# Two weight loads of the boot tied to a matmul, and 27 fewer spare instructions ahead of the first turn

## The chip, the cores and the metric

The kernel runs on one core of a Trainium2 chip. The core has a matmul engine (TensorE, PE in the profile, with its weight loads listed apart as PEld), VectorE (DVE), ScalarE (ACT), GpSimd (POOL), and SyncE (SP), which here only issues transfers. Sixteen DMA engines move the data that these engines ask for. The metric is the device time of one execution in microseconds; lower is better.

## The reference

Two blocks follow each other. The first is a linear recurrence over 768 steps for each of 4 x 8 heads of width 48, with a decay w for each channel:

```python
for t in range(S):
    cur = np.einsum('bhd,bhe->bhde', u[None] * kt, vt)
    y[:, :, t] = np.einsum('bhd,bhde->bhe', rt, state + cur)
    state = wt[:, :, :, None] * state + np.einsum('bhd,bhe->bhde', kt, vt)
```

Its output, as 3072 tokens of 384 numbers, goes through a layer of 2048 hidden units, all in float32:

```python
h = x @ w_in
g = h - np.tanh(h)
return g @ w_out
```

## The kernel before

The tokens are cut into eight blocks of 384 (four batches, two halves of the sequence). Within a block the recurrence is worked out by chunks of 64 steps: products of the decays by scans on VectorE (`behind` L387, `before` L376), scores within a chunk (`own`) and their decayed part (`earlier`) as small matmuls at L447, states from one chunk to the next (`update_1` L521 on TensorE, `update_2` L533 and L543 on VectorE), and then the block's result, from the scores (`from_scores`, L603) and from the states (`from_states`, L586). `result_out` (L636) copies the result to three tiles xT and one tile `late`, the fourth part, whose rows are then spread into holes that the three xT tiles have: six small transfers of 24 KB, called fills here (`fill_holes`, L643, `xT<-late`), three on SP's queue and three on GpSimd's for the first block, and all six on SP's for the others.

The second block of the reference then runs over 16 steps f: `hp` (L749, three matmuls of 128x384) makes the hidden values of 128 units, ScalarE copies them to `h` (L752), VectorE squares them (L778) or ScalarE does, two VectorE operations give g (L755, written to `sums` or `g`), and L826 or L864 multiplies with w_out into the accumulators `acc`. In the steps of one block, the recurrence of the next block is prepared, and the weights are converted: in the first block each of 16 pieces of weights arrives as 768 KB of 64-bit numbers (`raw`, L241), ScalarE takes three operations on it (L255) and VectorE one (L259). There are five buffers for `raw`.

Ahead of all this stands the boot (L963 to L1033), which does the recurrence of the first block alone, with nothing of the second block to fill TensorE. Its order on TensorE, ScalarE, VectorE and SP is the order of the code, written out by hand. The steps that matter here:

- SP first issues the loads of w, k and r in two halves, v, and three pieces of weights (L241).
- `turn` (L463 on) takes a number `ahead`: so many spare 16x16 matmuls (`passed`, L277), each two instructions, a weight load and a matmul, stand ahead of its six transposes (L471). The first turn has 97 of them. Nothing reads what they write.
- The fourth and fifth pieces of weights are the two loads of the change. Here the fourth is tied by `begin_behind` to the third of ScalarE's conversions of the first piece (`first_a[2]`, L255): SP's transfer waits for that operation. The fifth has no tie of its own and follows on SP's queue.
- `own`'s scores are masked by VectorE (L454), and `from_scores` for the first pair of heads follows on TensorE (L603, 48 matmul records).
- The first copies to `late` release the fills; `later.load("w")`, the next block's w, is tied to the first copy to xT2 and stands on SP's queue behind the three fills; the sixth piece of weights and the next block's k follow it.
- The fourth piece is converted from the end of the boot on (L255, at 27.63 us in the profile), the fifth in step f = 1 (at 33.30).

In the first steps of the loop, VectorE squares the first h (L778), scans the next block's w (L387), and then does the two operations L755 for the first g.

Of the kernel before, what the change touches and what calls it, by code (L numbers as in the profile page):

```python
# [50 lines left out]
B, H, S, D = 4, 8, 768, 48  # L51
P = 128
L = 64
# [3 lines left out]
NCP = NCH // 2  # L57
# [63 lines left out]
def kernel(  # L121
# [12 lines left out]
    nc = tc.nc  # L134
# [29 lines left out]
    start = const.tile([P, UP * NCH * LP], F32, name="start", tag="start")  # L164
# [32 lines left out]
    A = const.tile([P, 2, NPAIR, NCP, L], F32, name="scores", tag="scores")  # L197
# [41 lines left out]
    def load_weights(f, queue):  # L239
        raw = conv.tile([P, 2 * DM, 2], I32, name="raw", tag="raw")  # L240
        ins = queue.dma_start(out=raw, in_=weights[f].bitcast(I32).rearrange("p (n two) -> p n two", two=2))  # L241
        return f, raw, ins

    def convert(f, raw, _):

        lo, hi = raw[:, :, 0], raw[:, :, 1]
        a = w_sb[:, f, :].bitcast(I32)
        up = conv.tile([P, 2 * DM], I32, name="up", tag="up", bufs=4)  # L250
        low, high = (up.bitcast(t).rearrange("p (n two) -> p n two", two=2)[:, :, i]
                     for i, t in enumerate((U16, F16)))

        def scaled(to, of, scale, bias=0.0):
            return lambda: nc.scalar.activation(out=to, in_=of, func=AF.Copy, scale=scale, bias=bias)  # L255

        return [scaled(a.bitcast(F32), hi.bitcast(F32), HIGH_SCALE), scaled(high, hi.bitcast(F32), SIGN_SCALE),
                scaled(low, lo.bitcast(U32), *LOW)], [
                lambda: nc.vector.scalar_tensor_tensor(out=a, in0=a, scalar=3, in1=up, op0=ALU.logical_shift_left,  # L259
                                                       op1=ALU.bitwise_or)]  # L260

    def scratch(ps):
        return ps.tile([P, 2, BANK], F32, name="att", tag="att")

    def busy(to, n):

        by = ident.bitcast(BF16)
        for _ in range(n):
            nc.tensor.matmul(to, lhsT=by[:, 0:P], rhs=by.unsqueeze(1).to_broadcast([P, 2, 2 * P]), start=True,
                             stop=True, skip_group_check=True)  # L270
# [10 lines left out]
    class Block:  # L281
# [177 lines left out]
        def own(self, ps, p0):  # L459
            return self.masked(ps, "k", "r", masks["diagonal"], p0)  # L460

        def earlier(self, ps, p0):
            return self.masked(ps, "post", "pre", masks["above"], p0)  # L463
# [129 lines left out]
        def from_scores(self, yp, slots, first, last):  # L593
            for n, slot in slots:
                for p in reversed(slot):
                    for c in range(NCP):
                        for h in range(2):
                            for par in range(2):
                                toks = slice(64 * par, 64 * par + 64)
                                e0 = 64 * (h ^ (p % 2))  # L600
                                f0 = p * D2 + h * D
                                n0 = (n * NCP + c) * L
                                nc.tensor.matmul(yp[p % 2][e0:e0 + D, par, n0:n0 + L],  # L603
                                                 lhsT=self.v[toks, c, f0:f0 + D],
                                                 rhs=A[toks, h, p, c, :],
                                                 start=(first and n == slots[0][0] and c == 0),
                                                 stop=(last and (n, c) == (slots[-1][0], NCP - 1)),
                                                 skip_group_check=True)

        def results(self, ps):  # L610
            self.yp = [scratch(ps) for e in range(2)]
# [2 lines left out]
        def result(self, part, pairs, last=False, more=False, **how):  # L614

            if self.begun and not self.more:
                nc.tensor.wait_ge(fence, len(fences))
            slots = [(p // 2, [x for x in pairs if x // 2 == p // 2]) for p in pairs if p % 2 == 0]  # L620
            getattr(self, part)(self.yp, slots, not self.begun, last, **how)
            self.begun, self.more = True, more
            if not last and not more:
                nc.tensor.drain().then_inc(fence, 1)
                fences.append(None)

        def result_out(self, pairs, copy=None):

            copies = []
            for p in reversed(pairs):  # L630
                n = p // 2
                src = self.yp[p % 2][:, :, n * NCP * L:(n + 1) * NCP * L].rearrange("e a (c t) -> e c a t", t=L)
                dst = self.xT[p] if p < KC else self.late
                dst = dst.rearrange("e (c a t) -> e c a t", a=2, t=L)
                for rows in (slice(0, D), slice(64, 64 + D)) if copy else (slice(0, P),):
                    copies.append((copy or nc.scalar.copy)(out=dst[rows], in_=src[rows]))  # L636
            return copies[0]
# [108 lines left out]
    def first(xT, f, ps):  # L746
        hp = ps.tile([P, NB], F32, name="hp", tag="hp")
        for kc in reversed(range(KC)):
            nc.tensor.matmul(hp, lhsT=w_in_sb[:, f, kc, :], rhs=xT[kc],  # L749
                             start=(kc == KC - 1), stop=(kc == 0))  # L750
        h = dense.tile([P, NB], F32, name="h", tag="h")
        return h, nc.scalar.activation(out=h, in_=hp, func=AF.Copy, scale=1.0 / UPSCALE)  # L752
# [199 lines left out]
    def more_weights(queue):  # L952
        raws.append(load_weights(more_weights.n, queue))
        more_weights.n += 1
        return raws[-1][-1]
# [3 lines left out]
    def begin_behind(ins, dma):  # L959
        tc.add_manual_dep(dma.ins, ins.ins.name, mybir.DependencyInfo(  # L960
            mybir.DependencyClass.Sync, mybir.DependencyReason.DATA))

    def boot(ps, blk, later):  # L963
        h1, h2 = HALVES
        for p0 in HALVES:
            for name in ("w", "k", "r"):
                blk.load(name, p0, UP)
        blk.load_v()
        for _ in range(3):
            more_weights(nc.sync)  # L970

        def run(ops):
            for op in ops:
                op()

        both = (h1, h1 + 1), (h2, h2 + 1)
        blk.behind(h1, UP)
        blk.take_whole(h1, UP)
        blk.before(h1, UP)
        blk.times_behind(h1, UP)  # L980
        blk.times_u(h1, UP)
        blk.turn(ps, h1, ahead=97)
        own = blk.own(ps, h1)
        blk.times_before(h1, UP)
        earlier = blk.earlier(ps, h1)
        blk.bound(h1)
        blk.bound(h2)
        blk.behind(h2, UP)
        blk.take_whole(h2, UP)
        own()  # L990
        blk.times_behind(h2, UP)
        blk.times_u(h2, UP)
        blk.turn(ps, h2)
        own = blk.own(ps, h2)
        earlier()
        blk.before(h2, UP)
        blk.times_before(h2, UP)
        blk.update_1(ps)
        first_a, first_b = convert(*raws.pop(0))
        second_a, second_b = convert(*raws.pop(0))  # L1000
        third_a, third_b = convert(*raws.pop(0))
        run(first_a[:2])
        begin_behind(first_a[2](), more_weights(nc.sync))
        more_weights(nc.sync)
        own()
        blk.results(ps)
        blk.result("from_scores", both[0])
        blk.update_2()
        run(second_a)
        blk.result("from_states", ALL, cs=(0, 1), more=True)  # L1010
        earlier = blk.earlier(ps, h2)
        run(third_a[:2])
        blk.result("from_states", ALL, cs=(2,))
        earlier()
        idle = scratch(ps)[:, 0]
        busy(idle, 2)
        blk.result_out((3,), nc.scalar.copy)
        blk.fill_holes([nc.sync, nc.gpsimd])
        begin_behind(blk.result_out((2,), nc.scalar.copy), later.load("w"))
        more_weights(nc.sync)  # L1020
        run(first_b)
        blk.result("from_scores", both[1], True)
        busy(idle, 5)
        run(third_a[2:])
        blk.result_out((1,), nc.scalar.copy)
        blk.result_out((0,), nc.vector.tensor_copy)
        later.load("k")
        fourth_a, fourth_b = convert(*raws.pop(0))
        run(fourth_a[:1])
        run(second_b)  # L1030
        run(third_b)
        blk.held(0, NPAIR)
        return fourth_a[1:], fourth_b  # L1033
# [24 lines left out]
    for i, blk in enumerate(blocks):  # L1058
# [11 lines left out]
        phases, before, ahead, converted, loads = plan(i)  # L1070
# [3 lines left out]
        for f in range(NF):  # L1074
# [5 lines left out]
            h, made = first(here, f, ps_d)  # L1080
# [161 lines left out]
```

## Time and profile before

| | us |
|---|---|
| runs | 567.37, 567.84, 567.37 (median 567.37) |
| the profiled execution | 567.05 |
| its span, first to last instruction | 565.2 |
| boot: first hp (L749) begins | 27.87 |
| first unbroken stretch of TensorE begins (L826) | 40.72 |
| granted TensorE clock, mean | 0.999 |

The costliest groups of the page, with their line, engine, operation, output and inputs, count, busy us, mean ns of one, and the idle time before them:

```profile
L749 PE MATMUL hp<-xT,w_sb 128*128 128x384 f32 x768 | 270.1, 488 | 2.0 <-ACT h L752 1.4
L864 PE MATMUL acc<-forms,g 128*128 128x128 f32 x810 | 121.0, 277 | 0.5
L796 DVE TENSOR_TENSOR g<-g 128x256 f32<-128x256 f32 x225 | 95.4, 424 | 19.1 <-PE acc L864 0.5
```

TensorE sets the pace of the loop, and idles only a few microseconds of it. The boot is the part in which all engines wait for each other and for transfers. `SPq` in a row is SP's queue: the time that it took to issue a transfer, not the transfer's own. An instruction row with `x6` merges six neighbours, and a matmul of float32 is two records of weight load and two of matmul.

### The profile page before, as it was taken

How to read it: one execution, taken by the hardware profiler on the slowest of the kernel's cores; microseconds unless marked ns; L12 is line 12 of the kernel's file. 1: busy time of each engine (PE TensorE's matmuls, PEld its weight loads, DVE VectorE, ACT ScalarE, POOL GpSimd, SP SyncE). 2: the span in 40 equal slices, each digit the busy share in tenths (PEclk: the TensorE clock that was granted, in tenths of full speed). 3: DMA queues.
4: the chain of work that ended last, by engine and by line, in shares of the span. 5: the costliest groups of instructions: out<-in, count | busy, mean ns of one | idle time of the engine just before them, and what ended most of it. 6: DMA issues, size and time to landing. Idle time of an engine off the chain costs nothing.

```text
span 565.2 us, 13965 instructions
## 1 busy us (share of the span) xinstructions
PE 546.4 (97%) x5664; PEld 398.3 (70%) x5664; DVE 477.3 (84%) x926; ACT 376.8 (67%) x743; POOL 11.8 (2%) x40
## 2 busy tenths in 40 slices
PE   4889999999999999999999999999999999999996
PEld 4646666565665787877777777877877787787863
DVE  8888884799879989989999999989899998758673
ACT  3979893355337886588766886677865886566450
POOL 6100000000000000000000000000000000000000
PEclk9999999999999999999999999999999999999999
DMA  8596553244202532035302531126122320100101
GB/s 305 198 337 210 182 174 119 84 112 106 92 12 97 131 111 67 4 97 143 112 22 76 140 114 60 52 86 156 57 68 81 83 64 1 55 1 1 44 0 45
DMA packets 51268, 55.10 MB, mean 97 GB/s; under 512 B 21376, under 2 KB 49152, under 8 KB 51200
## 3 DMA queue, kind: packets, MB, share of 16 engines
q1 hardware_dynamic: 50960, 54.10, 31.6%
q8 instruction: 45, 0.74, 0.5%
q14 instruction: 23, 0.19, 0.1%
q0 software_dynamic: 96, 0.07, 0.1%
q10 hardware_dynamic: 144, 0.00, 0.0%
HBM read 43.55 MB, written 4.72 MB: 85 GB/s over the span
## 4 chain that ended last, share of the span: by engine, by line
PE 87%; DVE 6%; ACT 3%; DMA 2%; issue 1%; SPq 0%; DVEq 0%
PE hp L749 40%; PE acc L864 20%; PE acc L826 13%; PE att L864 5%; PE att L447 3%; PE att L586 2%; PE att L603 2%; PE att L521 2%; DVE g L796 1%; ACT up L255 1%; DMA r<-in_rT 1%; DMA w<-in_wT 1%; PE att L471 1%; DVE g L755 1%; DVE post L401 1%
## 5 line engine op out<-in xcount | busy, mean ns | idle before, releaser
L749 PE MATMUL hp<-xT,w_sb 128*128 128x384 f32 x768 | 270.1, 488 | 2.0 <-ACT h L752 1.4
L749 PEld LDWEIGHTS hp<-xT,w_sb 128*128 128x128 f32 x768 | 138.4, 190 | 81.8 <-ACT h L752 4.5
L752 ACT ACTIVATE h<-hp 128x384 f32<-128x384 f32 x128 | 62.8, 490 | 116.4 <-PE hp L749 114.7
L864 PE MATMUL acc<-forms,g 128*128 128x128 f32 x810 | 121.0, 277 | 0.5
L864 PEld LDWEIGHTS acc<-forms,g 128*128 128x128 f32 x810 | 109.1, 192 | 16.9 <-issue 1.2
L796 DVE TENSOR_TENSOR g<-g 128x256 f32<-128x256 f32 x225 | 95.4, 424 | 19.1 <-PE acc L864 0.5
L755 DVE SCALAR_TENSOR_TENSOR h<-h,s 128x384 f32<-128x384 f32 x128 | 70.3, 549 | 7.2 <-ACT s L770 6.6
L826 PE MATMUL acc<-w_sb,sums 128*128 128x384 f32 x192 | 68.1, 491 | 1.4 <-DVE sums L755 1.1
L755 DVE SCALAR_TENSOR_TENSOR g<-qa,h 128x384 f32<-128x384 f32 x96 | 53.6, 558 | 16.2 <-PE acc L864 2.7
L771 ACT ACTIVATE qa<-s,shift 128x384 f32<-128x384 f32 x90 | 55.4, 616 | 3.0
L773 ACT ACTIVATE junk<-s,shift 128x384 bf16<-128x384 f32 x90 | 54.0, 599 | 0.0
L826 PEld LDWEIGHTS acc<-w_sb,sums 128*128 128x128 f32 x192 | 35.7, 190 | 25.8 <-DVE sums L755 2.2
L770 ACT ACTIVATE s<-h 128x384 f32<-128x384 f32 x90 | 47.1, 523 | 2.8
L864 PE MATMUL acc<-w_sb,g 128*128 128x128 f32 x270 | 44.9, 275 | 0.0
L864 PEld LDWEIGHTS acc<-w_sb,g 128*128 128x128 f32 x270 | 37.4, 192 | 0.0
L781 ACT ACTIVATE qa<-s,shift 128x384 f32<-128x384 f32 x38 | 23.4, 617 | 19.3 <-DVE top L778 19.3
L255 ACT ACTIVATE up<-raw 128x768 f16<-128x768 f32 (+1 forms) x32 | 32.0, 1070 | 0.0
L755 DVE SCALAR_TENSOR_TENSOR sums<-qa,h 128x384 f32<-128x384 f32 x32 | 17.9, 558 | 15.6 <-ACT qa L781 12.4
L778 DVE CUSTOM_DVE_ANT_0 s<-h 128x384 f32<-128x384 f32 x38 | 21.0, 553 | 11.7 <-ACT h L752 11.7
L864 PE MATMUL att<-w_sb,g 128*128 128x128 f32 x180 | 30.2, 275 | 0.0
L864 PEld LDWEIGHTS att<-w_sb,g 128*128 128x128 f32 x180 | 26.4, 192 | 4.5
L387 DVE TENSOR_TENSOR_SCAN post<-w,seed 128x780 f32<-128x780 f32 x16 | 28.5, 1783 | 0.7 <-DMA w<-in_wT 0.6
(90 smaller groups left out, 549.3 us busy)
## 6 DMA issues: line engine op xcount, KB each, us to landing
raw<-in_weights SPq DMA_DIRECT2D x16, 768.0 KB, 4.4
w<-in_wT SPq DMA_DIRECT2D x7, 780.0 KB, 4.5
k<-in_kT SPq DMA_DIRECT2D x7, 768.0 KB, 4.4
r<-in_rT SPq DMA_DIRECT2D x7, 768.0 KB, 4.4
v_sb<-in_v SPq DMA_DIRECT2D x8, 576.0 KB, 4.3
k<-in_tokens SPq DMA_DIRECT2D x6, 576.0 KB, 3.9
r<-in_tokens SPq DMA_DIRECT2D x6, 576.0 KB, 4.8
out_y<-sums SPq DMA_DIRECT2D x15, 128.0 KB, 1.9
```

The source lines that it names most:

```text
L255: return lambda: nc.scalar.activation(out=to, in_=of, func=AF.Copy, scale=scale, bias=bias)
L387: return nc.vector.tensor_tensor_scan(out=back(t[:, 0:width]), data0=back(self.tile("w")[:, a:a + width]), data1=back(seed[:, 0:width]), i ...
L749: nc.tensor.matmul(hp, lhsT=w_in_sb[:, f, kc, :], rhs=xT[kc], start=(kc == KC - 1), stop=(kc == 0))
L752: return h, nc.scalar.activation(out=h, in_=hp, func=AF.Copy, scale=1.0 / UPSCALE)
L755: return lambda: nc.vector.scalar_tensor_tensor(out=out, in0=in0, scalar=scalar, in1=in1, op0=op0, op1=ALU.mult)
L770: nc.scalar.activation(out=s, in_=h, func=AF.Square)
L771: nc.scalar.activation(out=qa, in_=s, func=AF.Square, bias=shift[:, 4:5])
L773: nc.scalar.activation(out=junk[:, 0:NB], in_=s, func=AF.Relu, bias=shift[:, 5:6], accum_out=excess[:, at:at + 1])
L781: first = [lambda: nc.scalar.activation(out=qa, in_=s, func=AF.Square, bias=shift[:, 4:5])]
L796: return lambda: nc.vector.tensor_tensor(out=G[:, to:to + 2], in0=two(G, g_at(q, a0), g_at(q, a1)), in1=two(G, g_at(q, b0), g_at(q, b1)), ...
L826: nc.tensor.matmul(acc, lhsT=g[:, j * P:(j + 1) * P], rhs=w_out_sb[:, f, :], start=(f == self.first), stop=(f == NF - 1))
L864: nc.tensor.matmul(to, lhsT=G[:, g_at(q, a), :], rhs=rhs, start=start, stop=stop, skip_group_check=True)
```

## The change

The tie of the fourth weight load goes from ScalarE's third conversion to the last matmul of the first `from_scores`; for that, `from_scores` and `result` now return their last matmul. ScalarE's three conversions are the same ones in the same place. The two loads stand at the same place of SP's queue: behind the first three pieces, ahead of the fills. The first turn has 70 spare matmuls in place of 97.

```diff
-                                nc.tensor.matmul(yp[p % 2][e0:e0 + D, par, n0:n0 + L],
...
+                                done = nc.tensor.matmul(
+                                    yp[p % 2][e0:e0 + D, par, n0:n0 + L], lhsT=self.v[toks, c, f0:f0 + D],
...
+            return done
...
-            getattr(self, part)(self.yp, slots, not self.begun, last, **how)
+            done = getattr(self, part)(self.yp, slots, not self.begun, last, **how)
...
+            return done
...
-        blk.turn(ps, h1, ahead=97)
+        blk.turn(ps, h1, ahead=70)
...
-        run(first_a[:2])
-        begin_behind(first_a[2](), more_weights(nc.sync))
-        more_weights(nc.sync)
+        run(first_a)
         own()
         blk.results(ps)
-        blk.result("from_scores", both[0])
+        begin_behind(blk.result("from_scores", both[0]), more_weights(nc.sync))
+        more_weights(nc.sync)
```

In the built program TensorE has 54 instructions fewer, all of them ahead of the first turn, and the other engines have as many as before. On SP the fourth weight load waits for TensorE's counter in place of ScalarE's; the next block's k load, which named TensorE's counter too, no longer does, as the wait further up covers it.

More of the change, by code (lines that the diff above doesn't have):

```diff
@@ L602, in from_scores @@
                                 n0 = (n * NCP + c) * L
[L603 to L608, printed above, removed]
+                                done = nc.tensor.matmul(
+                                    yp[p % 2][e0:e0 + D, par, n0:n0 + L], lhsT=self.v[toks, c, f0:f0 + D],
+                                    rhs=A[toks, h, p, c, :], start=(first and n == slots[0][0] and c == 0),
+                                    stop=(last and (n, c) == (slots[-1][0], NCP - 1)), skip_group_check=True)
+            return done
         def results(self, ps):
```

## The prediction

> **What bounds the kernel now.** I read the page's totals first, then busy time by stage, then the chain of waits through the boot, then the order of time around the change.
>
> ```profile
> PE 546.4 (97%) x5664; PEld 398.3 (70%) x5664; DVE 477.3 (84%) x926; ACT 376.8 (67%) x743; POOL 11.8 (2%) x40
> ...
> q8 instruction: 45, 0.74, 0.5%
> ```
>
> ```profile
> 27.30:31.90 4.60, 3.86 (x13) 2.09 (x13) 2.63 (x7) 3.00 (x5) 0.00 (x0) 1.00 0.78 251
> 31.90:41.00 9.10, 7.85 (x25) 3.95 (x24) 8.36 (x13) 7.70 (x11) 0.00 (x0) 1.00 1.02 379
> 41.00:559.00 518.00, 515.25 (x5048) 376.29 (x5048) 441.52 (x865) 348.27 (x702) 0.80 (x12) 1.00 0.29 83
> ```
>
> From 41 us to the end TensorE is busy 515.25 of 518.00 us (first figure after each length) at a granted clock of 1.00. What happens there costs at most the 2.75 us left; everything else is decided by the moment at which that unbroken stretch starts. That moment is 40.72 us, and it is set by this chain:
>
> ```profile
> 27.29 4.54 DMA w<-in_wT
> ...
> 31.85 1.79 DVE post L387
> ...
> 40.11 0.57 DVE sums L755
> ...
> 40.72 2.20 PE acc L826 x6
> ```
>
> The load of the next block's w leaves SP at 27.29 and lands at 31.83; VectorE scans it (L387), and then works almost without a gap to the `sums` that L826 waits for. So a shift of L387's start is a shift of the end. The rows around the change:
>
> ```profile
> 17.39 1.97 ACT L255 ACTIVATE up<-raw 128x768 f16<-128x768 f32 x2
> 19.64 1.46 PE L603 MATMUL att<-scores,v_sb 64*48 64x64 f32 x48
> 24.57 2.61 SPq L643 DMA_DIRECT2D xT<-late  x3
> 27.29 0.52 SPq L330 DMA_DIRECT2D w<-in_wT  x1
> 27.87 2.17 PE L749 MATMUL hp<-xT,w_sb 128*128 128x384 f32 x6 [0.54 <-DMA xT<-late]
> 30.65 0.56 DVE L778 CUSTOM_DVE_ANT_0 s<-h 128x384 f32<-128x384 f32 x1 [1.30 <-ACT h L752]
> 31.85 1.78 DVE L387 TENSOR_TENSOR_SCAN post<-w,seed 128x780 f32<-128x780 f32 x1 [0.64 <-DMA w<-in_wT]
> ```
>
> L387 has two gates. One is the w load (31.83). The other is L778, ahead of it on VectorE, done at 31.21: it needs the first h, hence the first hp (27.87), hence the six small transfers xT<-late (the fills). The second gate has 0.64 us to spare.
>
> **The spare instructions.** 97 took 2.58 us, 27 ns each, so 27 fewer end 0.7 us sooner, at 3.9 instead of 4.65. TensorE then idles until 9.20, where it waits for VectorE's post (L401): gain 0. Without that idle stretch it would be 0.7. They leave no colder clock: the six turns of L471 take 1.54 us after 4.55 us of idling and 1.54 us again at 14.30 after 0.8.
>
> What they do change is where TensorE's instructions are fetched. The 45 packets of queue q8 are 0.74 MB, 16.4 KB each, and TensorE has 11,328 records: some 252 instructions a packet. Counting the built program's instructions against the packets' times, a packet starts about 1.05 us after TensorE has reached a place some 60 short of a multiple of 256. Each spare pair is two instructions, so every fetch comes 54 instructions later in the program. Fetch 4 was asked for near 22.4 us (L586) and will be near 22.8; fetch 5 moves from 30.8 past 40. [...] Here TensorE indeed never waits for one, but SP does:
>
> ```profile
> L643 SPq DMA_DIRECT2D xT<-late x3: 588/640/1297, 24.6 to 26.6; - x3
> ```
>
> ```profile
> q8 instruction: 1, 0.02, 57.6%
> ```
>
> The second line is from the DMA view of 25.2 to 25.3 us. The packet records give fetch 4 from 25.241 to 26.162; SP's second fill was issued at 25.252 and took 1.297 us where the median of 45 fills is 0.582. The same stretch to about 1.29 us recurs at 94.79 and 486.34, each with an instruction packet, and each ends 0.36 to 0.39 after the packet. So fetch 4 costs SP 0.715 us ahead of the w load.
>
> **The tie.** The fourth weight load was issued at 19.384, as ScalarE's third conversion ended (19.36). It will wait for the last of L603's 48 matmuls, 19.64 + 1.46 = 21.10; add the same 0.03: 21.13, later by 1.75. The fifth follows behind it. Behind both on SP stand the three fills, the w load, the sixth weights and k; SP is free again near 21.95, before the first fill's own release (24.54), so the queue's order costs nothing. The two loads landed at 23.89 and 25.75 and will land near 25.6 and 27.5; they are used at 27.63 and 33.30, so 2 and 5.8 us of cover hold, and 1.75 eats most of the first.
>
> **What they collide with.** DMA was 97% busy from 21.5 to 24.7. Fetch 4 waited 2.85 us from its asking and began 4 ns after its engine had finished its last weight packet. Its engine's fills come behind it: by the trace's landing records their last parts came at 27.44 (first SP fill), 27.26, 27.62 and 27.80 (GpSimd's), 1.1 to 1.6 after the fetch's end, and the first hp began 0.22 after 27.62, level with ScalarE's last xT copy (27.61). With the loads 1.75 later and fetch 4 asked for only 0.4 later, I expect it behind both loads again: start 25.24 + 1.75 = 26.99, end 27.92, fills from that engine near 29.1. No row shows this arrangement, so I bound it. If the engine's loads keep the whole 1.75, the first hp moves by 1.75. If they finish 0.5 earlier (fetch 3, which ran into their first packets at 20.14, moves to about 21.0, ahead of them) and queued fills follow each other in 0.35, it moves by 1.0. I take 1.4, nearer the upper row because that one is this very engine's.
>
> At the same time the second fill loses its 0.715 (the fetch is later), so w may leave at 26.58 and land near 31.1; if the fetch holds w's own issue to 27.92 + 0.37 = 28.29, it lands 4.02 after that (27.81 to 31.83): 32.3.
>
> **The sum.** L778 ends at 31.21 + 1.4 = 32.61, behind w in either case, so L387 starts 32.61 - 31.85 = 0.76 later. VectorE's stretch to `sums` is unchanged, and TensorE's own hps (over at 39.62, 1.10 of slack) are not in the way: +0.76. Against the profiled execution, span 565.2 and 1.85 around it, 567.05 becomes 567.81. The median of the runs is 0.32 above that execution: 567.37 + 0.76 = **568.1**. The bounds 1.0 and 1.75 give +0.36 to +1.10: 567.7 to 568.5.
>
> Later collisions are not charged. Fetches move by 0.4 to 5 us there, some onto other blocks' fills, but the stretch at 94.79 left no gap in TensorE at 98, where those fills are used.
>
> **Rivals.**
> 1. *The fetch slips between the two loads.* Fetch 4, at its engine near 23.85, goes between loads four and five: 24.9 to 25.8. The second fill is held as before (to 26.2) and w leaves near 26.9. That engine's share of load five, 8 packets of 234 ns, then ends near 27.7, its fills near 28.1, and they land 0.35 after that: hp later by about 0.65, L778 ends at 31.86: +0.01, 567.4. For it: fetch 4 did begin at an end of a load. Against it: fetch 5 was asked for near 30.8 and began at 34.67, deep in the k load, after a whole weight load and most of k; some 32 of an engine's packets passed first. [...]
> 2. *Nothing holds the fills (faster).* Fetch 4 is served in its usual 1.05 us, as fetches outside loads are. Then hp stays with ScalarE's copy at 27.61, SP gains its 0.715, and L387 starts at L778's end: -0.62, 566.75. For it: every fetch in a quiet stretch. Against it: fetch 1, with a wait of 3.5 in the first loads.
> 3. *The same, and the unexplained gap before `sums` goes too.* VectorE idles 0.56 at 34.31, and the profile names no wait; fetch 5 begins at 34.67 beside it and moves away. -0.62 - 0.56 = -1.18: 566.2. Only closeness in time speaks for it.
> 4. *The w load is caught instead of the second fill (clearly slower).* If the fetch's packet begins between 26.58 and 27.10, it holds w's issue itself; with the longest packet seen (1.43, at 305.3) behind a load end of 26.99, SP is free at 28.79, w lands at 32.81, and the fills of that engine land near 29.8, hp +2.1, L778 33.31: +1.0 to +1.5, 568.4 to 568.9. It decides once hp is later by more than 1.77. For it: my own start, 26.99, lies in that window. Against: the usual packet takes 1.0.
>
> **How the numbers follow.** Forecast 0.42; rival 1: 0.14; 2: 0.10; 3: 0.08; 4: 0.26. A measurement here can tell 0.2% (1.13 us) from no change: below 566.24 is faster, above 568.50 slower. Faster: rival 3 and 0.04 of rival 2, 0.12. Slower: rival 4, and 0.08 of the forecast for what its bounds leave out above, 0.34. Same: 0.34 + 0.14 + 0.06 = 0.54. For 8 in 10 the range runs from 566.4 (rival 2 in, most of 3 out) to 569.1 (rival 4 in, with 0.2 for its rounding); the forecast's own is 567.7 to 568.5.
>
> **What would show it.** Right: the two weight loads issued near 21.13; a q8 packet starting near 27 rather than 25.24; no second fill of 1.29; the first hp later by 1.0 to 1.75; L387 released by L778, not by w; the L826 gap ending near 41.5; the stretch after it unchanged. A q8 packet at 24.9 is rival 1; one at 23.9 with hp at 27.9, rival 2; that and no gap ahead of the first `sums`, rival 3; L387 waiting for w at 32.8, rival 4. Wrong altogether: an end that moves by another amount than L826's start.

## The result, and the profile after

| | before | after |
|---|---|---|
| runs on the same chip, median of 6 | 567.76 (567.37 to 568.30) | 571.12 (570.93 to 571.65) |
| ratio, 95% interval | | 1.0061 [1.0048, 1.0074] |
| the profiled execution | 567.05 | 571.19 |
| its span | 565.2 | 569.5 |
| first hp (L749) begins | 27.87 | 32.32 |
| first unbroken stretch of TensorE begins (L826) | 40.72 | 44.53 |

The change costs 3.4 us; 568.1 was forecast, and the time lies above the range (566.4 to 569.1). The two profiled executions are 4.14 apart because that of before is 0.7 faster than its median.

The page of the changed kernel, its totals and the fetch queue, which has as many packets as before:

```profile
PE 547.2 (96%) x5637; PEld 397.9 (70%) x5637; DVE 477.5 (84%) x926; ACT 376.9 (66%) x743; POOL 11.3 (2%) x40
...
q8 instruction: 45, 0.74, 0.5%
```

TensorE is busy 0.8 us longer with 27 matmuls fewer: something made it slower. Busy time by stage of the changed kernel (length, then busy us of PE, PEld, DVE, ACT, POOL, the granted clock, the DMA share, GB/s):

```profile
22.00:24.00 2.00, 1.01 (x55) 0.77 (x45) 1.87 (x4) 2.00 (x3) 0.13 (x2) 1.00 0.88 326
24.00:26.00 2.00, 0.00 (x0) 0.00 (x0) 0.96 (x2) 0.03 (x1) 0.00 (x0) 0.69 0.94 377
26.00:28.00 2.00, 1.29 (x25) 0.81 (x24) 0.00 (x0) 0.47 (x1) 0.00 (x0) 0.50 0.15 61
28.00:31.00 3.00, 2.91 (x52) 1.64 (x51) 0.43 (x1) 2.88 (x6) 1.58 (x3) 0.50 0.18 45
31.00:35.00 4.00, 3.81 (x12) 1.50 (x10) 2.60 (x5) 1.90 (x5) 0.00 (x0) 0.93 0.72 215
35.00:45.00 10.00, 9.17 (x28) 4.93 (x29) 9.16 (x17) 9.03 (x14) 0.00 (x0) 1.00 1.00 372
45.00:563.00 518.00, 515.16 (x5048) 376.36 (x5047) 441.43 (x863) 348.31 (x702) 0.79 (x12) 1.00 0.30 83
```

The long stretch at the end is what it was (515.16 of 518 us). New are two stages: from 24 to 26 TensorE does nothing at all, and from then to 31 its granted clock is 0.50. The order of time there:

```profile
20.24 0.54 PE L603 MATMUL att<-scores,v_sb 64*48 64x64 f32 x21 [0.49 <-issue]
20.83 0.80 SPq L241 DMA_DIRECT2D raw<-in_weights  x2
26.58 0.89 PE L586 MATMUL att<-pre,states 48*48 48x64 f32 x23 [3.46 <-issue]
28.52 2.23 SPq L643 DMA_DIRECT2D xT<-late  x3
30.86 0.52 SPq L330 DMA_DIRECT2D w<-in_wT  x1
32.32 2.17 PE L749 MATMUL hp<-xT,w_sb 128*128 128x384 f32 x6
35.10 0.56 DVE L778 CUSTOM_DVE_ANT_0 s<-h 128x384 f32<-128x384 f32 x1 [1.45 <-ACT h L752]
35.65 1.78 DVE L387 TENSOR_TENSOR_SCAN post<-w,seed 128x780 f32<-128x780 f32 x1
44.53 0.91 PE L826 MATMUL acc<-w_sb,sums 128*128 128x384 f32 x2 [0.56 <-DVE sums L755]
```

In the middle of L586, between the 9th and the 10th of its last 32 matmul records, TensorE stands still for 3.46 us. `<-issue` says that no semaphore that the profile shows ended the wait: no engine and no data transfer of the kernel. The chain of waits has the same hole, and behind it the way that the prediction followed:

```profile
23.12 3.46 issue
26.58 0.92 PE att L586 x23
...
30.44 1.77 PE att L269 x5
...
32.32 2.19 PE hp L749 x6
...
35.10 0.56 DVE s L778
...
35.67 1.78 DVE post L387
...
43.92 0.57 DVE sums L755
...
44.53 1.56 PE acc L826 x4
```

The sum of it: L586 ends at 26.58 + 0.89 = 27.47, before at 22.81 + 0.66 = 23.47: 4.00 later. Of this 3.46 are the hole; the rest is that its records took 1.57 in two parts instead of 0.66, less 0.37 by which TensorE was ahead when it began them. Another 0.45 come up to hp, where the five spare matmuls of L269 take 1.84 instead of 1.25 at a granted clock of 0.50: hp +4.45. L778 follows it, +4.45; L387 had 0.64 to spare and slips by 3.80; L826 by 3.81. The last 0.43 of the span's 4.24 come later, in the loop.

### The profile page after: what moved, and what is told of

Its sections match the earlier page's. It is cut to its first block, busy times and chain, and to the rows that moved or that the text cites. A ratio compares the mean times of both kernels' runs of the same rounds, so it can differ in the third digit from the quotient of the medians.

```text
span 569.5 us, 13910 instructions
## 1 busy us (share of the span) xinstructions
PE 547.2 (96%) x5637; PEld 397.9 (70%) x5637; DVE 477.5 (84%) x926; ACT 376.9 (66%) x743; POOL 11.3 (2%) x40
## 4 chain that ended last, share of the span: by engine, by line
PE 86%; DVE 8%; issue 2%; ACT 1%; DMA 1%; SPq 0%; DVEq 0%; ACTq 0%
PE hp L749 40%; PE acc L864 19%; PE acc L826 13%; PE att L864 5%; PE att L447 2%; PE att L586 2%; PE att L603 2%; PE att L521 2%; DVE g L796 1%; DMA r<-in_rT 1%; DVE states L533 1%; DVE states L543 1%; DVE g L755 1%; DVE pre L394 1%; DVE post L401 1%
## 5 line engine op out<-in xcount | busy, mean ns | idle before, releaser
L749 PE MATMUL hp<-xT,w_sb 128*128 128x384 f32 x768 | 270.1, 488 | 1.6 <-ACT h L752 1.4
L749 PEld LDWEIGHTS hp<-xT,w_sb 128*128 128x128 f32 x768 | 138.4, 190 | 81.3 <-ACT h L752 4.5
L796 DVE TENSOR_TENSOR g<-g 128x256 f32<-128x256 f32 x225 | 95.5, 424 | 19.1 <-PE acc L864 0.5
L826 PE MATMUL acc<-w_sb,sums 128*128 128x384 f32 x192 | 68.0, 490 | 0.8 <-DVE sums L755 0.6
L826 PEld LDWEIGHTS acc<-w_sb,sums 128*128 128x128 f32 x192 | 35.7, 190 | 25.1 <-DVE sums L755 1.2
L778 DVE CUSTOM_DVE_ANT_0 s<-h 128x384 f32<-128x384 f32 x38 | 21.0, 553 | 11.8 <-ACT h L752 11.8
L376 DVE TENSOR_TENSOR_SCAN pre<-w,start 128x780 f32<-128x780 f32 x16 | 28.5, 1783 | 0.6
```

Source lines behind the costliest of these rows:

```text
L376: return nc.vector.tensor_tensor_scan(out=self.tile("pre")[:, cols], data0=self.tile("w")[:, cols], data1=start[:, 0:n * NCH * LP], initia ...
L796: return lambda: nc.vector.tensor_tensor(out=G[:, to:to + 2], in0=two(G, g_at(q, a0), g_at(q, a1)), in1=two(G, g_at(q, b0), g_at(q, b1)), ...
L826: nc.tensor.matmul(acc, lhsT=g[:, j * P:(j + 1) * P], rhs=w_out_sb[:, f, :], start=(f == self.first), stop=(f == NF - 1))
```

## What the packets of instructions show

The instruction packets (queue q8) carry 16.4 KB each. In the changed kernel 256 records of TensorE, its sequencer's three among them, lie from one of the two waits below to the other, and 45 packets for its 11,274 records of weight loads and matmuls make some 251 each: I take a packet for a block of 256 instructions. I numbered TensorE's instructions in the built program (a float32 matmul is four) and matched them with the records. The hole stands between numbers 985 and 986, the short wait at 20.24 between 729 and 730; both are 256k - 38, and each time an instruction packet had ended 1.30 to 1.44 us before TensorE went on. The times of the packets had changed from the first one on. In the kernel before, packet 1 started at 7.97, ahead of the first turn (9.20). Stretch 0 to 9.2 us of the DMA view, before:

```profile
q8 instruction: 1, 0.02, 0.6%
```

The changed kernel's view of the same stretch has no such row; 13.0 to 19.5, where before has one packet, has two here:

```profile
q8 instruction: 2, 0.03, 2.0%
```

The packet records of all kernels of this study, from their one profiled execution each. "Enters 730" is the first record at or behind that instruction, "wait" TensorE's idle time at 986 (an entry under 0.1 is shown as 0):

| kernel | packet 1 | packet 2 | enters 730 | fourth weight load issued | packet 3 starts | its end to entry of 986 | wait | ratio of runs to before |
|---|---|---|---|---|---|---|---|---|
| before | 7.97 | 16.53 | 19.56 | 19.38 | 20.14 | 1.44 | 0 | 1 |
| after | 13.69 | 17.86 | 20.24 | 20.83 | 24.20 | 1.44 | 3.46 | 1.0061 |
| e1: tie, 97 | 7.80 | 16.45 | 19.00 | 19.96 | 20.12 | 1.41 | 0.2 | 0.9988 |
| e2: 70 alone | 13.35 | 18.13 | 20.51 | 19.47 | 25.19 | 1.44 | 4.55 | 1.0051 |
| e3: 70, later tie | 13.55 | 17.55 | 19.91 | 21.65 | 21.71 | 1.29 | 1.54 | 1.0024 |
| e4: tie, 84 | 12.83 | 16.44 | 19.14 | 19.97 | 22.82 | 1.48 | 2.97 | 1.0033 |
| e5: fifth later | 7.81 | 16.43 | 18.89 | 18.81 | 21.75 | 1.32 | 1.39 | 1.0012 |
| e6: w ahead of fifth | 8.01 | 16.53 | 19.06 | 18.98 | 22.03 | 1.50 | 1.66 | 1.0000 |
| e7: no tie | 7.88 | 19.13 | 21.72 | with the first pieces | 23.38 | 1.30 | 0.1 | 1.0035 |
| e8: tie, 130 | 7.54 | 16.13 | 18.67 | 20.10 | 19.81 | 1.53 | 0.97 | 1.0067 |
| e9: 70 and 27 | 13.54 | 17.22 | 19.53 | 19.49 | 22.33 | 1.38 | 2.49 | 1.0065 |
| e10: 110 | 7.60 | 16.01 | 19.12 | 19.48 | 19.76 | 1.37 | 0.3 | 1.0005 |
| e11: 70 wide | 13.41 | 17.04 | 19.40 | 18.39 | 24.02 | 1.41 | 4.01 | 1.0062 |
| e12: tie, 110 | 7.81 | 16.02 | 19.68 | 21.57 | 20.08 | 1.39 | 0.1 | 0.9996 |

Three things are read from it. First, the block at 986 is entered 1.29 to 1.53 us after packet 3's end, in the kernel before too (1.44). Its TensorE shows no wait there, but by this measure the block had no lead either: I read it as TensorE arriving about as the block did.

Second, in the ten kernels that show a wait at 730 (0.47 to 2.26 us), 730 is entered 2.31 to 2.70 us after packet 2 starts, and packet 3 starts 1.12 to 4.68 us after that entry. I read it so: TensorE needs packet 2 for 730, and packet 3 is asked for when TensorE gets there, so a late packet makes the next one late; the asking itself is in no record. (In before, e10 and e12, which don't wait at 730, packet 3 starts 0.40 to 0.64 us after the entry, so it was asked for sooner: by the 1.05 us that the prediction counted, near 19.1 in the kernel before, an estimate.)

Third, packet 3 starts at 19.76 to 20.14 where it is asked for ahead of the fourth weight load, and at 21.75 to 25.19 in the seven kernels where it is asked for behind it (after, e2, e4, e5, e6, e9, e11). Counted from the entry of 730, that is 2.80 to 4.68 us in these seven, and 1.12 to 1.80 in e1, e3, e7 and e8, which wait at 730 too but had no weight load put ahead of the packet just then. It didn't always come last in line. In e2 and e11 packet 3 starts as the last weight packets end (25.28 and 24.12). In the changed kernel it starts at 24.20, and 15 DMA engines are done with the weights by 26.62 while one goes on alone until 27.96: counted back at 234 ns a weight packet (the median of the 256 there, 16 for each engine), the engine that brought packet 3 had done about 4 of its 16 before it, an estimate.

Two rows seem to break this, after and e4, where 730 is entered ahead of the load. There 730 lies within L603, and only 42 or 70 instructions stand between it and a drain (L624 in the kernel before) that ends behind L603 (20.84 after 20.78 in the changed kernel), against 96 in e1. Their packets fit an asking only behind that drain, which is when the load goes out (after) or just about (e4); that is inferred, as the trace doesn't show the asking. e3 has the 42 too, but its loads go out only 0.07 before its packet starts, and don't delay it.

## The experiments

The theories stated with the first kernels were: the fetch is caught behind the weight loads (the count of spare instructions costs); the tie's lateness costs; TensorE is colder with fewer spare matmuls. The runs of the kernel before scatter on every chip (566.7 to 573.1 over the 18 beside e9 and e10), so the ratios with their intervals decide, not the medians alone.

**e1_tie_97: the change's tie, with the 97 spare matmuls of before.**

```diff
-        blk.turn(ps, h1, ahead=70)
+        blk.turn(ps, h1, ahead=97)
```

> The tie alone: the loads wait for the matmul, and the spare matmuls stay at 97. Theory F (an instruction fetch that queues behind the weight loads starves TensorE): the block of instructions that holds the first L603 is entered near 19.5 us, so the third fetch begins before 21 us, ahead of the loads issued near 21.1; no stall in L586, TensorE goes on at 23.1; 0 to 1.2 us over before (the later fills, as I had priced them). Theory T (the loads' lateness itself costs the time, by fills and the w load): as slow as the change, +3 us or more.

568.27 (12 runs) against 567.95, ratio 0.9988 [0.9966, 1.0009]. The tie alone costs nothing measurable. Its order of time has a wait of its own, for packet 2, ahead of L603, and none in L586:

```profile
19.00 0.89 PE L603 MATMUL att<-scores,v_sb 64*48 64x64 f32 x48 [1.48 <-issue]
```

That wait moves nothing, since L586 waits for VectorE's states behind it (0.30 us). And its stages from 22 us on:

```profile
22.00:24.00 2.00, 2.00 (x76) 1.95 (x68) 1.52 (x4) 1.22 (x2) 0.13 (x2) 0.50 0.96 390
24.00:26.00 2.00, 1.86 (x31) 0.81 (x26) 1.20 (x2) 1.70 (x4) 0.99 (x2) 0.50 0.73 275
26.00:28.00 2.00, 1.91 (x35) 1.06 (x28) 0.71 (x2) 1.94 (x4) 0.59 (x2) 0.50 0.32 89
```

The granted clock is 0.50 here as in the changed kernel, yet this execution took 568.49. So the halved clock by itself isn't what costs the 3.4 us.

**e2_spare_70: the kernel before with 70, without the tie.**

```diff
-        blk.turn(ps, h1, ahead=97)
+        blk.turn(ps, h1, ahead=70)
```

> The count alone: 70 spare matmuls, the loads tied to ScalarE's third conversion as before. Theory F: the third fetch is asked for near 20.2 us, after the loads were issued at 19.4, and stands behind the fourth load: it begins at 22.8 us or later, and TensorE stalls in L586 for 2 to 3.5 us; +2.5 to +4.5 us. Theory T: nothing is late, +0 to 0.5 us. A third theory, W (27 spare matmuls less leave TensorE colder in the boot, without any fetch): +0.5 to 2 us, with slower matmuls and no gap.

571.84, ratio 1.0051 [1.0032, 1.0069]: the whole loss comes with the number. Order of time:

```profile
20.51 0.54 PE L603 MATMUL att<-scores,v_sb 64*48 64x64 f32 x21 [0.71 <-issue]
27.57 0.89 PE L586 MATMUL att<-pre,states 48*48 48x64 f32 x23 [4.55 <-issue]
```

The waits stand at the same two instructions as in the changed kernel, and the second is longer: the loads are issued 1.4 us earlier, and packet 3 comes a microsecond later.

**e3_tie_states: 70, the loads tied to the last matmul of the first `from_states` instead.**

```diff
-        begin_behind(blk.result("from_scores", both[0]), more_weights(nc.sync))
-        more_weights(nc.sync)
...
-        blk.result("from_states", ALL, cs=(0, 1), more=True)
+        begin_behind(blk.result("from_states", ALL, cs=(0, 1), more=True), more_weights(nc.sync))
+        more_weights(nc.sync)
```

> The change with the two loads tied still later, to the last matmul of the first from_states (about 22 us). Theory F: the third fetch, asked for near 20.2, begins near 21.3, ahead of the loads; the stall in L586 is 0.6 us or less and the clock stays up; +0.3 to +2 us over before (loads land near 28.4, so the fills and w come later than in the change). Theory T: loads later still, so slower than the change: +3.5 us or more.

569.80, ratio 1.0024 [1.0002, 1.0045]: about half of the loss goes. With packet 3 at 21.71 and the loads issued from 21.65 on, the wait in L586 is 1.54:

```profile
24.35 0.67 PE L586 MATMUL att<-pre,states 48*48 48x64 f32 x23 [1.54 <-issue]
```

But this profiled execution took 571.77, near the top of its 12 runs (568.81 to 572.16), and its last stretch of TensorE begins at 45.04, later than the changed kernel's 44.53. The chain of waits names what else is late (this kernel's lines lie two further down, so L751 is hp):

```profile
26.45 4.25 DMA xT<-late
30.94 4.14 PE hp L751 x6
```

A fill took 4.25 us to land, as the two loads landed only at 27.94 and 30.18, and the first hp took 4.14 instead of 2.19 at a granted clock of 0.50 (24.65 to 34.89). So the loads' lateness does cost time when they are tied this late, which is theory T's way if not its size. How the wait and the fills share the loss of the 12 runs, one profile doesn't tell.

**e4_spare_84: the changed kernel with 84 (`ahead=84`).**

> The change with 84 spare matmuls for 70: block ends come 28 instructions earlier in the program than in the change. Theory F: the second fetch no longer starves L603, the third is asked for some 0.4 us sooner and begins near 21 us, ahead of the loads: no long stall, 0 to 1.2 us over before. Theory T: the tie is the same, so as slow as the change. Theory W: between before and the change, +1.5 us or so.

570.76, ratio 1.0033 [1.0013, 1.0052]. A miss: I had expected no long wait, and there is one of 2.97, in L447. I had looked at the order of packet 3 and the loads alone, and hadn't seen that packet 1 is late here too (12.83).

**e5_fifth_later, e6_w_first: the kernel before, with the fifth weight load moved behind the next block's w, and with the two exchanged.** Both were tries at a faster version.

```diff
         begin_behind(first_a[2](), more_weights(nc.sync))
-        more_weights(nc.sync)
...
         begin_behind(blk.result_out((2,), nc.scalar.copy), later.load("w"))
+        more_weights(nc.sync)
```

```diff
-        more_weights(nc.sync)
+        later.load("w")
...
-        begin_behind(blk.result_out((2,), nc.scalar.copy), later.load("w"))
+        begin_behind(blk.result_out((2,), nc.scalar.copy), more_weights(nc.sync))
```

> Before, with only the fifth weight load moved behind the next block's w on SP (97 spare, the fourth tied as before). Theory F: the fourth fetch meets one load in place of two and begins near 23.5 us in place of 25.2; the second fill is no longer held (0.58 for 1.30 us), w leaves some 0.7 us sooner, L387 starts at L778's end: -0.3 to -0.7 us, about the edge of what can be told. Theory T (it is the loads' lateness that costs): the fifth load is later by 8 us, so slower than before.

> Before, with the next block's w and the fifth weight load changing places on SP (97 spare). The w lands near 25 us, so L387 no longer waits for it: -0.6 us at most, as L778 ends at 31.2. The third fetch is asked for before the loads as in before: no stall. Theory T would have it faster by the same, so this one looks for a version that is better, and tells how much of the end w sets.

568.31 and 568.77 against 568.05, ratios 1.0012 [0.9993, 1.0031] and 1.0000 [0.9978, 1.0022]: no gain. In both profiled executions (569.63 and 569.77) the fourth load happened to be issued 0.08 us before TensorE entered 730, and packet 3 came at 21.75 and 22.03, with waits of 1.39 and 1.66. The kernel before stands close to this edge: its load goes out at 19.38, and the packet that starts at 20.14 was asked for near 19.1, by the estimate above. That is a likely source of its scatter; it wasn't tried.

**e7_no_tie: the kernel before, with all five weight loads at its start.**

```diff
-        for _ in range(3):
+        for _ in range(5):
             more_weights(nc.sync)
...
-        begin_behind(first_a[2](), more_weights(nc.sync))
-        more_weights(nc.sync)
+        first_a[2]()
```

> Before without any tie: all five weight loads issued at once at the start (97 spare). Theory F: the DMA engines are busy until 21 us, the second fetch stands behind loads, and TensorE stalls at the first L603 for 2 to 4 us: +2 to +5 us. Theory T: the loads come sooner, so nothing can be late for them: 0 to -0.6 us.

570.53, ratio 1.0035 [1.0020, 1.0050]. Now packet 2 is the one behind the loads (19.13 instead of 16.53), and TensorE waits at 730 instead of 986:

```profile
21.73 1.53 PE L603 MATMUL att<-scores,v_sb 64*48 64x64 f32 x48 [2.26 <-issue]
```

So the wait moves with the caught packet, to the first instruction of that packet's block. Two of its 12 runs had a mean granted clock of 0.999 and took 570.31 and 570.38, so this loss is there without the lower clock too.

**e8_spare_130: the changed kernel with 130 (`ahead=130`).**

> The change with 130 spare matmuls for 70: block ends come 120 instructions earlier in the program than in the change, 66 earlier than in before. Theory F: the third fetch is asked for in L521, ahead of TensorE's drain and of the loads; it begins by 20.5 us; no stall over 1 us: 0 to 1.2 us over before. Theory W (few spare matmuls leave TensorE colder): faster than before, -0.5 us or more. Theory T: as slow as the change.

571.86, ratio 1.0067 [1.0046, 1.0088], and a miss. The boot is much as expected: packet 3 at 19.81, a wait of 0.97 at 986 and not of 3, L826's stretch from 41.91. Two more waits stand at block ends, 1.56 us at 730 and 0.52 at 1242, the latter 1.28 after packet 4's end. Measured against before's profile its h copies (128 of them, counted from 0) are 1.2 us late in numbers 8 to 40, but 2.2 in number 64 and 3.3 from number 80 on. So about 2 us are lost in the loop, which the changed kernel doesn't lose (+3.84 in number 8, +4.24 at the end). The blocks end at other instructions there, but no wait of TensorE behind 45 us follows a packet's end by 1.3 to 1.5 us as in the boot, and the longest that before doesn't have, 0.45 at 283.80, is for VectorE's states (L543). What costs the 2 us was not found.

**e9_moved_27 and e10_spare_110: the kernel before with 70, and 27 more ahead of the second turn; and with 110.** The first puts every instruction behind the second turn at its number of before.

```diff
-        blk.turn(ps, h1, ahead=97)
+        blk.turn(ps, h1, ahead=70)
...
-        blk.turn(ps, h2)
+        blk.turn(ps, h2, ahead=27)
```

> The kernel before, with 70 spare matmuls ahead of the first turn and the other 27 ahead of the second turn. Fetch theory (what counts is where TensorE's blocks of 256 instructions end, not how many spare ones warm it): all instructions from the second turn on stand at the same place in the program as before, so the third instruction packet is asked for ahead of the weight loads, starts near 20.1 us, and no idle stretch of over 1.5 us stands inside L586 or L447 behind 21 us; 567.5 to 569, ratio 0.998 to 1.002. Theory of a colder TensorE (70 ahead of the first turn is too few): the clock falls as with 70 alone, 571 to 572, ratio 1.005.

> The kernel before, with its tie, and 110 spare matmuls in place of 97: 26 instructions more, the third block of 256 ends within L521, ahead of the first scores. Fetch theory: the third packet is asked for ahead of the weight loads, as with 97 and 130; L586 has no idle stretch over 1.5 us; the boot ends as in the kernel before, L826's stretch starts within 1.5 us of 40.7. In the loop the blocks end at other places, as with 130, which lost 2 us there in its one profile: from 567.5 to 570. Theory that only the number of spare instructions counts, more being warmer: at or below the kernel before, 567 to 568.

e9: 571.30 against 567.34, ratio 1.0065 [1.0045, 1.0085]. This went against the fetch theory as I had it, and is what a colder TensorE would give:

```profile
24.64 0.80 PE L447 MATMUL att<-pre,post 48*64 48x64 f32 x18 [2.49 <-issue]
```

The packets showed what the theory lacked. Packet 1 is at 13.54 as with 70, not at 7.97. Number 196, 60 short of 256, is reached at 4.45 in the kernel before, near the end of its 97 spare matmuls, so the first fetch falls into the idle time ahead of the turn. With 70 they end some 54 numbers sooner, and 196 is reached behind the turn, at 11.15 (11.40 in the changed kernel). The lateness is handed on: packet 2 at 17.22 instead of 16.53, entry of 730 at 19.53 just behind the load (19.49), packet 3 at 22.33. e10, where packet 1 is early: 567.52, ratio 1.0005 [0.9991, 1.0020], packet 3 at 19.76, a wait of 0.3. More spare matmuls don't help further.

**e11_wide_70 and e12_tie_110.** e11 tells the fetch from the warmth: 70 spare matmuls of 128 columns keep TensorE busy longer than 97 of 16, with 54 instructions fewer. e12 is the changed kernel with 110.

```diff
-            nc.tensor.matmul(to[0:16, 0:16], lhsT=by, rhs=by, start=True, stop=True, skip_group_check=True)
+            nc.tensor.matmul(to[0:16, 0:128], lhsT=by, rhs=ident.bitcast(BF16)[:, 0:128], start=True, stop=True, skip_group_check=True)
...
-        blk.turn(ps, h1, ahead=97)
+        blk.turn(ps, h1, ahead=70)
```

> The kernel before, with 70 spare matmuls of 128 columns in place of 97 of 16: TensorE works at least as long ahead of the first turn as in the kernel before, but has 54 instructions fewer, so that its first instruction packet is not asked for until the turn itself, as with 70 narrow ones. Fetch theory, with the chain from the first packet on: packets at 13 to 14, 17 to 18.5 and 22 to 25.5 us, an idle stretch over 2 us in L586 or L447 behind 21 us, 570 to 572.5. Theory of a colder TensorE: it is as warm as before, so the third packet starts near 20.1, no such stretch, 567 to 568.5.

> The changed kernel with 110 spare matmuls in place of 70, so with the tie to the last matmul of the first scores. Fetch theory: the first packet starts in TensorE's idle time before 9.2 us, the third ahead of the weight loads (19.7 to 20.3), no idle stretch over 1.5 us in L586 or L447 behind 21 us; the tie itself costs at most its own lateness at the first hp, so 567 to 569. Theory that the tie alone costs: 570 to 572, as the changed kernel.

e11: 571.37 against 567.73, ratio 1.0062 [1.0038, 1.0086], packet 1 at 13.41, packet 3 at 24.02. Order of time:

```profile
2.07 5.53 PE L277 MATMUL att<-ident 128*16 128x128 bf16 x70 [2.07 <-POOL ident masks.py:199]
9.24 0.88 PE L471 MATMUL att<-ident,post 128*128 128x128 f32 x6 [1.65 <-DVE post L401]
26.38 0.89 PE L586 MATMUL att<-pre,states 48*48 48x64 f32 x23 [4.01 <-issue]
```

TensorE worked until 7.6 us and did the first turn in 0.88 where before took 1.54: it was faster there than in the kernel before, and the kernel lost as much as the changed one. The theory of the colder TensorE falls. What goes with packet 1's time here is the number of instructions that TensorE gets through before its first long wait: with 97 spare matmuls or more it starts at 7.54 to 8.01, with 84 or 70 at 12.83 to 13.69. e12: 568.41 against 567.73, ratio 0.9996 [0.9976, 1.0016]. With an early packet 1 the tie costs nothing measurable again, though its loads leave at 21.57. The first hp of e10, then of e12:

```profile
29.28 2.17 PE L749 MATMUL hp<-xT,w_sb 128*128 128x384 f32 x6 [1.88 <-DMA xT<-late]
```

```profile
29.87 2.17 PE L749 MATMUL hp<-xT,w_sb 128*128 128x384 f32 x6 [2.02 <-DVE holds L423]
```

Both wait for fills (in e12 the last of GpSimd's landed at 29.80, 0.07 before hp). Against before's profile hp is 1.41 and 2.00 later, and L826's stretch 0.70 (41.42) and 1.30 (42.02). That leaves about 0.6 us for the tie, from one execution of each, which is less than the runs resolve. No version here is measurably faster than the kernel before.

## Why the prediction was wrong, and where it was right

- **The spare instructions: the failing step.** Half of it held: the 27 matmuls are hidden in the idle time ahead of the first turn. What failed is "gain 0" as the whole price of 27 fewer (TensorE stood still for 3.46 us here, for 4.55 in e2), and the sentence "Here TensorE indeed never waits for one". Two readings led there. First, "every fetch comes 54 instructions later" was turned into 0.4 us for fetch 4 and 0.9 for fetch 3, and what it does to fetch 1 was not worked out. For packet 1 those 54 instructions straddle TensorE's wait for VectorE's post, and cost 5.72 us (7.97 to 13.69). From there packet 2 came 1.33 later and packet 3, which I had put at "about 21.0, ahead of them" (the loads), at 24.20. Second, I took a trace without a gap for a TensorE far ahead of its needs. It was at the limit: packet 3 ended at 21.07, its block was entered at 22.51, 1.44 later, and where TensorE visibly waits the figure is 1.29 to 1.53. Both were there to be read before: the packets' times and the count of instructions were in my hands, and I asked only when a packet was fetched, not when its block was needed.
- **The tie: right, and no cause.** Loads at 20.83 (forecast 21.13; L603 ended earlier). They landed at 26.53 and 28.40, later than the 25.6 and 27.5 forecast, and were first used at 31.59 and 37.75: the cover held. e1 and e12 put the tie itself at nothing that can be measured: their intervals end at 1.0009 and 1.0016, and the 0.76 that was forecast would be 1.0013.
- **What they collide with: not what moved hp here.** Packet 4 did move off (28.80; I had said 26.99), and no second fill took 1.29 (the longest of 45 took 0.953). hp was to slip by 1.4, bounds 1.0 to 1.75; it slipped by 4.45, because of TensorE's own wait and not of the fills. The bounds were rows of the wrong mechanism, so they held nothing. The chain that was forecast, late fills and hp behind them, is seen where packet 3 is not caught: hp +1.41 in e10, without the tie, and +2.00 in e12.
- **The sum: the form was right.** L387 starts with the end of L778 and not for w; hp's slip less 0.64 is 3.81, measured 3.80; L826 follows with 3.81. The gap ending near 41.5 ended at 44.53.
- **The rivals.** None is what happened. All of them start from how fetch 4 meets the loads; the fetch that was caught is the third. It did slip in between weight packets, as rival 1 had it for the fourth, and was late all the same. "Later collisions are not charged" hides 0.43 in the profiled pair.
- **The clock.** "They leave no colder clock" is right as to the 27 spare matmuls: the first turn takes 1.54 us with 70 as with 97. That 1.54 is the turn's time at full speed was not shown: in e11 it takes 0.88. The granted clock fell 1.65 us into the 3.46 us of waiting, which I had not foreseen.

## What to carry to other kernels

An instruction count is a position: before adding or removing instructions, even idle ones, number the engine's instructions, lay the fetch packets beside them, and note for each block how long after its packet's end the engine enters it; where it was some 1.5 us (1.29 to 1.53 in these profiles), there was no cover, gap or no gap. A long wait of TensorE put off its next fetch too: what stood ahead of the wait decided whether the next block came during it or after it (packet 1 at 7.97 or at 13.69). Two loads of 768 KB issued ahead of a fetch went with a delay of microseconds (packet 3 at 22.33 to 25.19 in e2, e9 and e11, against 20.14 before).

## What the hardware showed that I had not expected

- In twelve of the fourteen profiles TensorE waits 0.2 us or more at number 730 or 986, and goes on 1.29 to 1.53 us after the end of one packet of 256 instructions. I infer that it held no block beyond the one that it ran; no record shows what it holds.
- Queued loads of 768 or 780 KB (one in e5, two elsewhere) went with a fetch that is later by microseconds: behind them packet 3 starts 2.80 to 4.68 us after the entry of 730, against 1.12 to 1.80 in the four other kernels that wait there.
- In the changed kernel the granted clock was 0.50 for 6.83 us (24.77 to 31.60 by the clock records), from 1.65 us into the wait of 3.46 on. In e1 such a window began at 20.12, in e2 at 25.41. In the kernel before the first record starts at 20.95 and the windows show 1.00 ahead of it, though L521 took 2.76 us there against 1.79 in the changed kernel (17.44 to 19.23, recorded as 1.00 from 17.95 on). I take it that a 1.00 ahead of the first record is no measurement.
